# Seven staged weight slices, a third engine for a normalization, split first loads, an early Exp, and a new written order

## The chip, the cores and the metric

The kernel runs on one core of a Trainium2 chip. The core has five engines that run side by side, each through its own list of instructions in order: TensorE (PE in the rows; PEld is its loading of weights), VectorE (DVE), ScalarE (ACT), GpSimd (POOL) and SyncE (SP), which here does nothing but issue DMAs. They meet at semaphores. The metric is the time of one execution on the device in microseconds (us), the median of several runs.

## The reference, cut to what matters

```python
# q, k, v: (4 batches, 12 heads, 448 rows, 64), float32
scores = q @ k.T / 8, causal mask, softmax       # per batch and head
x = attn @ v, heads put side by side             # (4, 448, 768)
mixed = real(fft(fft(x, axis=1), axis=2))
u = x + mixed
un = (u - mean(u)) / sqrt(var(u) + 1e-6)         # per row of 768
out = u + maximum(un @ w_ch1, 0) @ w_ch2         # w_ch1: 768 x 3072, w_ch2: 3072 x 768
```

The weights arrive as 64-bit floats; each pair of 32-bit words is made into one float32 on the chip.

## The kernel before

The program is a list of some 4,300 units: a matmul group, a copy, a DMA issue and so on. The functions of `tile_kernel` add the units; each names what it reads and writes. Two tables written out by hand then fix everything: `RUN` is the order in which the units are issued, and `BY` gives each unit's engine (P, V, S, G, D for PE, DVE, ACT, POOL and a DMA on SP's queue). `BANK` and `BUF` give the PSUM bank or buffer of each new tile. So each engine's list is its part of `RUN`, and each waits only where a unit needs what another engine has not finished.

The work falls in three stages that overlap:

- **Attention and DFT** (to about 260 us). `attend` takes one pair of heads at a time, 24 pairs: load `raw` (q and k) and `v`; scale q to `qs`; masks and scores into PSUM (PE, lines 581 and 588); row minima `mn` (DVE, 600); exponentials `p` with their sums (ACT, 608); reciprocals `ri` (DVE, 616 and 620); normalizing `p` (638, 640, 642 on ACT, DVE or POOL); four groups of transposes (PE, 654), each copied to `pa`; then the product with v (PE, 664), copied to `xt`. After six pairs a batch is whole: `fold` makes sums and differences `f` of `xt` (DVE, POOL), and `dft` multiplies them by tables (PE, 722 and 739), adds `xt` transposed (PE, 765), which gives `u` (DVE, 775). `un`, the normalized `u`, is made at line 801 from the row's mean and from a factor that POOL works out in two small operations (791 and 792), transposed (811) and written to DRAM.
- **First layer** (F1, 1,512 matmuls at line 1014, to about 547 us). Strassen's scheme: seven products of half-size blocks. `weights` turns raw 64-bit weights into float32 `w32` (ACT 833, 837, 850; DVE 856, 860); `split` makes a high and a low part of each block (copies at 487 and 489, differences at 876), `combine` the sums of blocks (882). Three matmuls (high-high, high-low, low-high) stand for one. Results go to DRAM.
- **Second layer** (F2, 1,764 matmuls at line 1184, to the end). Twelve slices of w_ch2 pass in the same way. Those listed in `EARLY` are split during F1 already and kept in DRAM (`w2`, stores at 1144); F2 only fetches them. The others are made during F2. DVE adds each product to `acc` or `ue` (1200).

At the start eleven dummy matmuls (`warm`, line 502) run while the first data come in. `W_FROM = 10` lets the first weight load start once the v of pair 10 has been loaded.

## Time and profile before

| | us |
|---|---|
| median of 3 runs (lowest to highest) | 862.75 (862.38 to 864.58) |
| the profiled execution, its own time | 862.93 |
| its span, first to last instruction | 861.2 |
| PE busy in the span | 846.0 |
| DVE, ACT, POOL busy | 726.9, 542.9, 452.9 |

Between the span and the execution's own time lie 1.7 us. PE is busy 98% of the span. Matmuls are pipelined and their ends are modelled, so a busy PE may still lose a little between matmuls; the number of matmuls in equal windows tells of that. [...]

### The profile page before, as it was taken

The page shows a single profiled execution, that of the slowest core. Times are in us where ns is not written, and L with a number is a line of the kernel's source. Part 1 is how long each engine was busy: PE and PEld are TensorE (multiplying, and loading weights), DVE is VectorE, ACT ScalarE, POOL GpSimd, SP SyncE. Part 2 cuts the span into 40 slices and gives each one's busy share as a digit, 9 for nine tenths or more (in the row PEclk, how much of TensorE's full clock was granted, in tenths as well). Part 3 has the DMA queues.
Part 4 walks back from the last instruction along what each step waited for, and adds up shares of the span by engine and source line. Part 5 has one row for each costly group of instructions (what it writes and reads, how often), then busy time and mean ns, then how long its engine had stood idle before and what let it go on. Part 6 is the DMA issues. An engine that isn't in the chain of part 4 may idle for free. (4 is left out here: it accounts for less than half of the span.)

```text
span 861.2 us, 15758 instructions
## 1 busy us (share of the span) xinstructions
PE 846.0 (98%) x5407; PEld 754.7 (88%) x5407; DVE 726.9 (84%) x1335; ACT 542.9 (63%) x1120; POOL 452.9 (53%) x466
## 2 busy tenths in 40 slices
PE   8999999999999999999999999999999999999998
PEld 4677677686788899899999988999999999999998
DVE  5889999888999996898877659899799999987653
ACT  5888999979788977787777456584443421332220
POOL 1654756668270234345453342446646666797675
PEclk9999999999999999999999999999999999999999
DMA  6535847656596687888778668574474385447332
GB/s 225 171 118 180 299 135 214 210 171 182 168 294 215 210 276 264 259 274 282 261 247 275 223 205 280 186 245 140 137 228 131 119 275 157 129 122 236 115 133 91
DMA packets 121359, 174.02 MB, mean 202 GB/s; under 512 B 21696, under 2 KB 98240, under 8 KB 121280
## 3 DMA queue, kind: packets, MB, share of 16 engines
q1 hardware_dynamic: 121280, 173.03, 62.3%
q8 instruction: 42, 0.69, 0.3%
q14 instruction: 37, 0.30, 0.1%
HBM read 112.83 MB, written 60.16 MB: 201 GB/s over the span
## 5 line engine op out<-in xcount | busy, mean ns | idle before, releaser
L1184 PE MATMUL psum<-wa,w 128*128 128x384 f32 x1050 | 208.6, 336 | 0.5 <-DVE acc L1200 0.3
L1184 PEld LDWEIGHTS psum<-wa,w 128*128 128x128 f32 x1050 | 184.0, 188 | 1.7 <-issue 0.6
L1184 PE MATMUL psum<-wb,w 128*128 128x384 f32 x714 | 149.6, 336 | 0.0
L1184 PEld LDWEIGHTS psum<-wb,w 128*128 128x128 f32 x714 | 125.9, 188 | 0.2 <-DVE ue L1200 0.2
L1014 PE MATMUL psum<-0t,w 128*128 128x448 f32 x432 | 107.9, 366 | 2.1 <-DVE c L489 0.8
L1014 PE MATMUL psum<-1t,w 128*128 128x448 f32 x432 | 102.4, 363 | 0.9 <-ACT c L487 0.5
L850 ACT ACTIVATE w<-w 128x768 int8<-128x768 f32 x48 | 94.4, 1967 | 0.5
L876 POOL TENSOR_TENSOR w<-ws,w 128x384 fp32r<-128x384 f32 x57 | 64.5, 1139 | 53.4 <-DVE w L489 24.2
L608 ACT ACTIVATE p<-psum,mn 128x256 f32<-128x256 f32 (+3 forms) x168 | 83.2, 510 | 10.4 <-DVE mn L600 10.0
L1014 PEld LDWEIGHTS psum<-0t,w 128*128 128x128 f32 x432 | 79.9, 188 | 10.9 <-ACT c L487 3.3
L1014 PEld LDWEIGHTS psum<-1t,w 128*128 128x128 f32 x432 | 80.4, 187 | 8.2 <-ACT c L487 1.3
L487 ACT CAST w<-us 128x384 fp32r<-128x384 f32 x65 | 32.5, 516 | 77.5 <-PE psum L1184 49.0
L1200 DVE TENSOR_TENSOR acc<-psum,acc 128x384 f32<-128x384 f32 x96 | 51.1, 550 | 26.1 <-PE psum L1184 25.2
L487 ACT CAST w<-ws 128x384 fp32r<-128x384 f32 x81 | 39.9, 515 | 52.1 <-DVE ws L882 22.2
L876 POOL TENSOR_TENSOR w<-us,w 128x384 fp32r<-128x384 f32 x45 | 52.5, 1174 | 36.3 <-ACT w L487 22.4
L600 DVE TENSOR_REDUCE mn<-psum 128x1 f32<-128x448 f32 (+3 forms) x96 | 62.0, 665 | 10.6 <-PE psum L588 8.1
L588 PE MATMUL psum<-raw,qs 64*128 64x384 f32 (+3 forms) x336 | 66.5, 430 | 0.1
L642 POOL TENSOR_TENSOR p<-p,ri 128x128 f32<-128x128 f32 (+3 forms) x61 | 37.5, 635 | 39.7 <-DVE ri L620 35.2
L1040 DVE TENSOR_TENSOR c<-psum,c 128x448 f32<-128x448 f32 x69 | 42.7, 620 | 15.8 <-PE psum L1014 8.9
L1014 PE MATMUL psum<-ue,w 128*128 128x448 f32 x216 | 54.1, 365 | 0.0
L654 PEld LDWEIGHTS psum<-cst,p 128*128 128x128 f32 x384 | 42.6, 141 | 12.6 <-issue 3.8
L860 DVE SCALAR_TENSOR_TENSOR w<-w,w 128x768 uint32<-128x768 uint32 x48 | 49.6, 1033 | 4.5 <-ACT w L850 3.9
(195 smaller groups left out, 1844.7 us busy)
## 6 DMA issues: line engine op xcount, KB each, us to landing
w<-in_w_dram SPq DMA_DIRECT2D x48, 768.0 KB, 4.9
h<-c SPq DMA_DIRECT2D x93, 224.0 KB, 2.9
w<-us SPq DMA_DIRECT2D x84, 192.0 KB, 2.7
raw<-in_qk_dram SPq DMA_DIRECT2D x23, 480.0 KB, 4.4
c<-h SPq DMA_DIRECT2D x56, 192.0 KB, 2.9
us<-h SPq DMA_DIRECT2D x56, 192.0 KB, 3.4
wa<-w SPq DMA_DIRECT2D x23, 384.0 KB, 5.1
wb<-w SPq DMA_DIRECT2D x19, 384.0 KB, 4.9
```

What stands on the lines that cost most here:

```text
L487: nc.scalar.copy(out=out, in_=in_)
L588: nc.tensor.matmul(out=T[ps][:, at[r]:at[r] + n], lhsT=T[qs][s, q0:q0 + 128], rhs=T[raw][s, QW:QW + n], start=False, stop=y == len(rows) - ...
L600: nc.vector.tensor_reduce(out=z, in_=x, axis=AX, op=ALU.min)
L608: nc.scalar.activation(out=T[pb][:, PO[rr]:PO[rr] + n], in_=T[ps][:, c0:c0 + n], func=ACTF.Exp, scale=-1.0, bias=T[mn][:, rr:rr + 1], accu ...
L654: nc.tensor.transpose(T[ps][:, 128 * k:128 * k + 128], T[pb][:, e:e + 128], T["cst", 0][:, 0:128])
L850: nc.scalar.activation(out=T[w].bitcast(I8)[:, :, 3], in_=T[w][:, :, 1].bitcast(F32), func=ACTF.Prelu, scale=SIGN_SCALE, alpha=SIGN_ALPHA)
L860: nc.vector.scalar_tensor_tensor(out=T[w32], in0=T[w32], scalar=3, in1=T[w][:, :, int(join)], op0=ALU.logical_shift_left, op1=ALU.bitwise_or)
L876: (nc.gpsimd if eng == "G" else nc.vector).tensor_tensor(out=lo(), in0=src(), in1=hi(), op=ALU.subtract)
L1014: nc.tensor.matmul(out=T[ps][:, 0:S], lhsT=w[:, a, t], rhs=T[us[t]][:, b], start=first and k == 0, stop=last and k == 8, skip_group_check= ...
L1040: nc.vector.tensor_tensor(out=T[z], in0=T[ps][:, 0:S], in1=T[z], op=ALU.add)
L1184: nc.tensor.matmul(out=T[ps][:, 0:384], lhsT=T[hb][:, a, y], rhs=T[z][:, b], start=first and y + v == 0, stop=last and y == n - 1 and v == ...
L1200: nc.vector.tensor_tensor(out=x, in0=T[ps][:, 0:384], in1=x, op=ALU.add)
```

## The change

- `EARLY` has a seventh slice, 5, in F1: it is split there, stored in 14 DMAs and fetched in seven during F2. It had been made in F2.
- `un` may be made on ACT, as one Identity with a scale and a bias per row. In the new `BY` 10 of the 16 are: two of batch 0, one of batch 1, three of batch 2, all four of batch 3. For it POOL works out two more numbers per row, for all 16: four small operations in place of two.
- The first pair's q and k come in four pieces and its q is scaled in two; the constants come, and are cast, in two pieces.
- An Exp of one number per partition stands first on ACT. Nothing uses its result.
- `W_FROM` is 0: the first weight load may start after the first v.
- `RUN`, `BY`, `BANK` and `BUF` are new throughout. PE does the same 1,005 units. Counted in the tables, DVE has 1,311 units (1,335 before), ACT 949 (951), POOL 474 (445), and SP 612 DMAs (588).

```diff
@@ constants of the plan
-ALONE, WIN, REST, EARLY, JOIN = 3, 3, (0,) * 7, (0, 3, 6, 8, 9, 11), ()
+ALONE, WIN, REST, EARLY, JOIN = 3, 3, (0,) * 7, (0, 3, 5, 6, 8, 9, 11), ()
-C_FROM, W_FROM, N_WARM = 0, 10, 11
+C_FROM, W_FROM, N_WARM = 0, 0, 11
@@ RUN (BY, BANK and BUF alike)
-    0, 6, 2, 5, 43, 89, 1, 7, 126, 8, 3, 9, 16, 10, 13, 20, 45, 14, 17, 11, 46, 172, 44, 12, 15, 91, 49, 18, 21, 19,
+    0, 4, 2, 6, 9, 8, 7, 10, 1, 11, 49, 95, 133, 96, 12, 5, 3, 13, 15, 14, 22, 19, 16, 26, 18, 21, 51, 132, 23, 50,
...
@@ consts
-        def f():
-            nc.sync.dma_start(out=T["cst", 0], in_=cc)
-        add("D", dma(128 * 4 * CW), -2498.5, f, wr=[("cst", 0)], phase="A")
-
-        def f(eng):
-            copy(eng, T["bfc", 0], T["cst", 0])
-        add(("S", "V", "G"), (acts(CW), dve(CW, 1.92), gps(CW)), -1898, f, rd=[("cst", 0)], wr=[("bfc", 0)], phase="A")
+        for key, c0, c1, p in (("b", 128, CW, -2498.5), ("a", 0, 128, -2300)):
+            def f(c0=c0, c1=c1):
+                nc.sync.dma_start(out=T["cst", 0][:, c0:c1], in_=cc[:, c0:c1])
+            add("D", dma(512 * (c1 - c0)), p, f, wr=[("cst", 0, key)], phase="A")
+
+            def f(eng, c0=c0, c1=c1):
+                copy(eng, T["bfc", 0][:, c0:c1], T["cst", 0][:, c0:c1])
+            n = c1 - c0
+            add(("S", "V", "G"), (acts(n), dve(n, 1.92), gps(n)), p + 600, f, rd=[("cst", 0, key)], wr=[("bfc", 0, key)], phase="A")
-        add("G", 80, 1000, f, wr=[("eps", 0)], phase="A")
+            nc.gpsimd.memset(T["eps", 0][:, 2:3], -1.0)
+        add("G", 80, -2600, f, wr=[("eps", 0)], phase="A")
+
+        def f():
+            nc.scalar.activation(out=T["eps", 0][:, 3:4], in_=T["eps", 0][:, 0:1], func=ACTF.Exp)
+        add("S", 1500, -2599, f, rd=[("eps", 0)], wr=[("eps", 0, "e")], phase="A")
@@ attend, loading and scaling
-            load(QW, QW + S, [(*raw, "k")], base - 2500)
-            load(0, QW, [(*raw, "q")], base - 2499)
+            load(QW, QW + 256, [(*raw, "k")], base - 2500)
+            load(0, 256, [(*raw, "q")], base - 2499)
+            load(256, QW, [(*raw, "q1")], base - 2498)
+            load(QW + 256, QW + S, [(*raw, "k1")], base - 2497)
-            load(0, QW + S, [(*raw, "q"), (*raw, "k")], base - 2500)
+            load(0, QW + S, [(*raw, z) for z in ("q", "k", "q1", "k1")], base - 2500)
-        def f(eng):
-            if eng == "S":
-                nc.scalar.mul(T[qs], T[raw][:, 0:QW], -0.125)
-            else:
-                (nc.gpsimd if eng == "G" else nc.vector).tensor_scalar(
-                    out=T[qs], in0=T[raw][:, 0:QW], scalar1=-0.125, scalar2=None, op0=ALU.mult)
-        add(("S", "V", "G"), (acts(QW), dve(QW, 1.92), gps(QW) + 216), sp, f, rd=[(*raw, "q")], wr=[qs], phase="A")
+        for k, (c0, c1) in enumerate(((0, 256), (256, QW)) if i == 0 else ((0, QW),)):
+            def f(eng, c0=c0, c1=c1):
+                x, z = T[raw][:, c0:c1], T[qs][:, c0:c1]
+                if eng == "S":
+                    nc.scalar.mul(z, x, -0.125)
+                else:
+                    (nc.gpsimd if eng == "G" else nc.vector).tensor_scalar(out=z, in0=x, scalar1=-0.125, scalar2=None, op0=ALU.mult)
+            n = c1 - c0
+            add(("S", "V", "G"), (acts(n), dve(n, 1.92), gps(n) + 216), sp + k, f, rd=[(*raw, "q1" if k else "q"), *([] if i == 0 else [(*raw, "q1")])],
+                wr=[(*qs, k)], phase="A")
@@ dft, normalization
-                    nc.gpsimd.tensor_tensor(out=T[st6][0:w, 14:15], in0=T[st6][0:w, 13:14], in1=T["eps", 0][0:w, 0:1], op=ALU.add)
-                    nc.gpsimd.tensor_tensor(out=T[st6][0:w, 14:15], in0=T[st6][0:w, 14:15], in1=T["eps", 0][0:w, 1:2], op=ALU.pow)
-                add("G", 785, pr[0], f, rd=[mv, ("eps", 0)], wr=[rs], phase="Q")
+                    r = T[st6][0:w, 14:15]
+                    nc.gpsimd.tensor_tensor(out=r, in0=T[st6][0:w, 13:14], in1=T["eps", 0][0:w, 0:1], op=ALU.add)
+                    nc.gpsimd.tensor_tensor(out=r, in0=r, in1=T["eps", 0][0:w, 1:2], op=ALU.pow)
+                    nc.gpsimd.tensor_tensor(out=T[st6][0:w, 15:16], in0=T[st6][0:w, 12:13], in1=r, op=ALU.mult)
+                    nc.gpsimd.tensor_tensor(out=T[st6][0:w, 15:16], in0=T[st6][0:w, 15:16], in1=T["eps", 0][0:w, 2:3], op=ALU.mult)
+                add("G", 1300, pr[0], f, rd=[mv, ("eps", 0)], wr=[rs], phase="Q")
+                    if eng == "S":
+                        nc.scalar.activation(
+                            out=T[un][0:w], in_=T[u][0:w], func=ACTF.Identity, scale=T[st6][0:w, 14:15], bias=T[st6][0:w, 15:16])
+                        return
-                add(("V", "G"), (590, 3150), pr[0], f, rd=[*ua, mv, rs], wr=[un], phase="Q")
+                add(("V", "G", "S"), (590, 3150, acts(768) + 93), pr[0], f, rd=[*ua, mv, rs], wr=[un], phase="Q")
```

Where the order moves things, three places. The first is the start of ACT's list: up to the first pair's exponentials (`p`, from scores in `psum` and minima `mn`).

Before:

```order
L608 ACT_TABLE_LOAD
L608 ACTIVATE p,sum<-psum,mn 128x256
L608 ACTIVATE p,sum<-psum,mn 128x128 x2
L608 ACTIVATE p,sum<-psum,mn 128x256
L608 ACTIVATE p,sum<-psum,mn 128x384 x2
L608 ACTIVATE p,sum<-psum,mn 128x448 x2
L638 ACTIVATE p<-p,ri 128x256
```

With the change:

```order
L524 ACT_TABLE_LOAD
L524 ACTIVATE eps<-eps 128x1
L567 ACTIVATE qs<-raw 128x256 x2
L622 ACTIVATE p,sum<-psum,mn 128x128
L622 ACTIVATE p,sum<-psum,mn 128x256 x2
L622 ACTIVATE p,sum<-psum,mn 128x128
L622 ACTIVATE p,sum<-psum,mn 128x384
L622 ACTIVATE p,sum<-psum,mn 128x448
```

The table load stood in front of the first exponential, behind the minima that this one waits for; now it stands in front of the Exp on `eps`, which waits for a POOL memset alone, and two scalings of q follow it.

The second place is on PE, around the product with v of pair 8 (`pa,v`), behind the last transposes of that pair (`cst,p`); the L581 rows of the masks that stand between are left out.

Before:

```order
L588 MATMUL psum<-raw,qs 128x128 x2
L588 MATMUL psum<-raw,qs 128x256 x2
L654 MATMUL psum<-cst,p 128x128 x12
...
L588 MATMUL psum<-raw,qs 128x448
L654 MATMUL psum<-cst,p 128x128 x4
L664 MATMUL psum<-pa,v 64x384 x2
L664 MATMUL psum<-pa,v 64x64 x2
```

With the change:

```order
L668 MATMUL psum<-cst,p 128x128 x12
L832 MATMUL psum<-cst,un 128x112 x3
...
L601 MATMUL psum<-raw,qs 128x128 x2
L601 MATMUL psum<-raw,qs 128x256 x2
L678 MATMUL psum<-pa,v 64x384 x2
L678 MATMUL psum<-pa,v 64x64 x2
```

One group of four transposes stood just ahead of the product with v. Now transposes of `un` and a whole unit of scores (`raw,qs`, with its masks) stand between.

The third is on PE too, from behind the last product with v (pair 23; with the change, from behind a first group of `un` transposes too) to the first DFT matmul of batch 3 (`cd,f`), which needs that product's copies `xt` and their sums `f`; `ue,w` and `0t,w` are F1 matmuls.

Before:

```order
L1014 MATMUL psum<-ue_2425,w_1026 128x448 x3
L765 MATMUL psum<-cst,xt_2372 112x128 x3
L1014 MATMUL psum<-0t_3022,w_2942 128x448 x3
L1014 MATMUL psum<-ue_2612,w_1026 128x448 x3
L1014 MATMUL psum<-0t_3027,w_2942 128x448 x3
L765 MATMUL psum<-cst,xt_2372 113x128 x3
L811 MATMUL psum<-cst,un 128x112 x3
L1014 MATMUL psum<-0t_3035,w_2942 128x448 x3
L722 MATMUL psum<-cd,f_2729 113x194
```

With the change:

```order
L1035 MATMUL psum<-ue_1697,w_916 128x448 x3
L1035 MATMUL psum<-ue_2582,w_906 128x448 x3
L832 MATMUL psum<-cst,un 128x112 x3
L1035 MATMUL psum<-ue_2466,w_916 128x448 x3
L1035 MATMUL psum<-ue_2588,w_916 128x448 x3
L1035 MATMUL psum<-0t_3033,w_2985 128x448 x3
L779 MATMUL psum<-cst,xt_2434 112x128 x6
L779 MATMUL psum<-cst,xt_2434 113x128 x3
L1035 MATMUL psum<-0t_3043,w_2985 128x448 x3
L1035 MATMUL psum<-0t_3054,w_2985 128x448 x3
L1035 MATMUL psum<-0t_3068,w_2936 128x448 x3
L736 MATMUL psum<-cd,f_2774 113x194
```

Ahead of the first transposes of `xt` (`cst,xt`) stood one group of three F1 matmuls; now five such groups and two of `un` transposes stand there, and up to the first `cd,f` there are eight groups of three F1 matmuls where there were five.

## Rows read from the trace of the kernel before

**Rows 1.** Page, part 1: engine, busy us (share of the span), instructions.

```profile
PE 846.0 (98%) x5407; PEld 754.7 (88%) x5407; DVE 726.9 (84%) x1335; ACT 542.9 (63%) x1120; POOL 452.9 (53%) x466
```

**Rows 2.** Windows: us, then busy PE, PEld, DVE, ACT, POOL, clock, DMA share, GB/s.

```profile
0.00:16.00 16.00, 13.23 (x77) 6.20 (x78) 7.89 (x20) 7.29 (x24) 0.59 (x5) 1.00 0.81 274
16.00:45.00 29.00, 28.16 (x307) 19.77 (x307) 25.28 (x51) 25.39 (x88) 16.59 (x24) 1.00 0.47 149
...
80.00:124.00 44.00, 42.00 (x439) 29.23 (x438) 42.51 (x97) 41.78 (x118) 27.75 (x39) 1.00 0.67 224
...
214.00:262.00 48.00, 45.85 (x292) 38.33 (x291) 46.14 (x93) 40.25 (x80) 22.18 (x25) 1.00 0.77 236
262.00:300.00 38.00, 37.21 (x179) 32.61 (x178) 37.00 (x69) 34.36 (x61) 6.36 (x5) 1.00 0.62 202
300.00:500.00 200.00, 199.05 (x991) 184.61 (x990) 158.96 (x271) 141.26 (x190) 80.86 (x73) 1.00 0.78 260
500.00:560.00 60.00, 58.39 (x294) 53.60 (x294) 48.84 (x90) 37.33 (x60) 22.55 (x21) 1.00 0.74 230
560.00:850.00 290.00, 289.50 (x1666) 288.07 (x1665) 245.36 (x414) 106.71 (x203) 195.56 (x167) 1.00 0.52 162
850.00:861.20 11.20, 7.56 (x44) 7.24 (x42) 3.61 (x7) 0.00 (x0) 1.04 (x2) 0.94 0.39 140
```

**Rows 3.** Timeline, first 16 us: start, us, engine, line, operation, count, idle before.

```profile
1.18 4.87 PE L502 MATMUL psum<-xt 128*128 128x512 bf16 x11 [1.18 <-DVE xt L496]
...
6.59 0.52 PEld L588 LDWEIGHTS psum<-raw,qs 64*128 64x128 f32 x8 [0.32 <-DMA raw<-in_qk_dram]
...
8.70 1.28 ACT L608 ACT_TABLE_LOAD   x1 [8.70 <-DVE mn L600]
...
10.96 0.30 PE L581 MATMUL psum<-bfc 64*128 64x128 bf16 x6 [0.64 <-ACT p L608]
...
13.50 0.19 PE L581 MATMUL psum<-bfc 128*128 128x64 bf16 x1 [0.67 <-ACT p L608]
```

**Rows 4.** Waits of PE, 80 to 125 us: total, times, longest.

```profile
PE psum L664 <- ACT pa L487: 0.5, 1, 0.5
...
PE psum L664 <- DVE pa L489: 0.4, 1, 0.4
```

**Rows 5.** Timeline of PE, 218 to 262 us.

```profile
220.18 1.98 PE L664 MATMUL psum<-pa,v 128*64 128x384 f32 x28
...
224.05 0.59 PE L765 MATMUL psum<-cst,xt 128*112 128x128 f32 x3 [1.08 <-ACT xt L487]
...
228.76 2.54 PE L722 MATMUL psum<-cd,f 128*113 128x194 f32 x14 [0.40 <-DVE f L701]
```

**Rows 6.** Windows of 20 us, two of them.

```profile
260.00:280.00 20.00, 19.39 (x95) 17.15 (x94) 19.67 (x39) 17.26 (x30) 1.47 (x1) 1.00 0.63 203
360.00:380.00 20.00, 20.00 (x102) 18.58 (x101) 16.97 (x28) 16.79 (x24) 7.66 (x7) 1.00 0.83 267
```

**Rows 7.** Tile un: count, ns min/median/max, first and last start.

```profile
L801 DVE TENSOR_SCALAR un<-u,st x16: 642/673/1370, 73.0 to 254.8; 112x768 f32<-112x768 f32 x12, 113x768 f32<-113x768 f32 x4
```

**Rows 8.** Line 791, the same columns.

```profile
L791 POOL TENSOR_TENSOR st<-st,eps x16: 191/192/845, 70.8 to 253.8; 112x1 f32<-112x1 f32 x12, 113x1 f32<-113x1 f32 x4
```

**Rows 9.** Lines by form, ACT and DVE: count, busy us, mean ns, idle before.

```profile
L833 ACT ACTIVATE w<-w 128x768 f32<-128x768 f32 x48 | 44.1, 919 | 12.2 <-POOL ws L882 3.3 <-DVE ws L882 3.2 <-POOL w L876 2.1
...
L860 DVE SCALAR_TENSOR_TENSOR w<-w,w 128x768 uint32<-128x768 uint32 x48 | 49.6, 1033 | 4.5 <-ACT w L850 3.9
```

**Rows 10.** Line 876: count, ns min/median/max.

```profile
L876 DVE TENSOR_TENSOR w<-ws,w x59: 543/552/1385, 218.4 to 824.2; 128x384 fp32r<-128x384 f32 x59
```

**Rows 11.** Line 1200, the same columns.

```profile
L1200 DVE TENSOR_TENSOR acc<-psum,acc x96: 541/548/559, 592.6 to 857.6; 128x384 f32<-128x384 f32 x96
```

**Rows 12.** Waits of the DMA queue: total, times, longest.

```profile
SPq L1144 <- POOL w L876: 75.7, 24, 7.7
```

More of the change, by code (lines that the diff above doesn't have):

```diff
@@ new lines @@
+BUF = (
+    "13000200021121213000011011101221020120112012121002103100120212110020110000102211222113021100301000210201110121"
+    "12220001113100020113012120320101211011100023102210010200013211121011110120001311103200101111232302220132011221"
+    "03100110100120112110121003010201121200001311021020030231013213201004010223124501230123012301213020202671321001"
+    "13012301230121100460104275320111403062124073120121102202012010312003120312321403050126104311201112100410302132"
+    "01002231103752121267500210012120010313202130130111043021142276200112201203501231052611042301032032102311201201"
+    "01203400147210311000323413210230120221100212035220160507110413213030123023021120001120023014126721301130321223"
+    "101230201200001400032154063521201212240220712203205402611720012003a46511301872e92fd1304gc0b6319123410761015012"
+    "13021101224103762120013512407640102232005217123113015012720034310052165c8bgae10044d370f287cb0ga410213510720140"
+    "23065106732520133020621721023451004372101104620513064122074105210102032461257302e256f9d0312131196354db80ce3011"
+    "0212054760021233512234134021072026504200223511037104310107620524371021361106043232120710101545af7g2ab12007044c"
+    "8g9e162f5d3101373212617311002620156140221123720156433200221100727620035121405201202730236410021337216574310022"
+    "502601040110061253167")
@@ L590, in f @@
                             start=False, stop=y == len(rows) - 1, skip_group_check=True)
-            add("PE", SC_COST[0 if tail else len(rows)], p0, f, rd=[qs, (*raw, "k"), ("bfc", 0)], wr=banks, phase="A", mode="F" if tail else "H")
+            add("PE", SC_COST[0 if tail else len(rows)], p0, f, rd=[*([(*qs, 0), (*raw, "k")] if i or k == 0 else [(*qs, 0), (*qs, 1), (*raw, "k"), (*raw, "k1")]), *([(*raw, "k1")] if i else []),
+                ("bfc", 0, "b"), *([("bfc", 0, "a")] if tail else [])], wr=banks, phase="A", mode="F" if tail else "H")
             for y, r in enumerate(rows):
@@ L654, in f @@
                     nc.tensor.transpose(T[ps][:, 128 * k:128 * k + 128], T[pb][:, e:e + 128], T["cst", 0][:, 0:128])
-            add("PE", TR_COST, p0, f, rd=[*[(*pb, r, "n") for r in {r for r, _ in blocks}], ("cst", 0)], wr=[ps], phase="A")
+            add("PE", TR_COST, p0, f, rd=[*[(*pb, r, "n") for r in {r for r, _ in blocks}], ("cst", 0, "a")], wr=[ps], phase="A")
             def f(eng, ps=ps, g=g):
```

102 lines of the change are left out of this document (45 added, 57 removed), and 457 rows, old and new, of the table RUN.

## Prediction

> **What bounds the kernel now.** I read the page's part 1 first: PE is busy 846.0 of the span's 861.2 us, so all that a new order can win back is PE's idle time, 15.2 us, and what PE loses between matmuls while it counts as busy [rows 1]. The arithmetic on PE is unchanged, 1,005 units.
>
> Windows by stage say where the idle time lies (stretch less PE busy): 2.8 us in the first 16, 0.8 from 16 to 45, 2.0 from 80 to 124, 2.2 from 214 to 262, 0.8 from 262 to 300, 0.95 from 300 to 500, 1.6 from 500 to 560, 0.5 from 560 to 850, and 3.6 at the end [rows 2]. The reader is to see two things. The stretches that lose most are those where another engine is full: ACT 41.78 and DVE 42.51 of 44 from 80 to 124, DVE 46.14 of 48 and 37.00 of 38 from 214 to 300. And F2 is nearly free of loss, though DVE is busy there for 245.36 of 290.
>
> Busy hides more. A window of 20 us in mid F1 holds 102 matmuls, 0.196 us each; the one from 260 to 280 holds 95, so it loses 7 x 0.196 = 1.4 us, where its idle time is 0.61 [rows 6]. The 179 matmuls from 262 to 300 fill 35.1 of 38 us: 2.9 lost, 0.8 of it as idle [rows 2].
>
> The end of 3.6 us (last product, last sum, last store) is written as before, and the wait of 1.18 ahead of the dummies too [rows 3].
>
> **The change, part by part.**
>
> *The early Exp.* ACT's first work was the table load, 1.28 us from 8.70 on, behind the first minima, with the exponentials behind it [rows 3]. From 8.70 to 16 ACT is busy 7.29 of 7.30 us, so what it starts late it ends late. PE waits for those exponentials twice, 0.64 and 0.67 [rows 3]. Now the load waits for a memset only and lies under the dummies, which hold PE until 6.05. Worth 1.28 at most by this way; the normalization of the first pair also passes DVE, whose new order puts one more minimum ahead of it, so I take 1.2, with bounds 0.5 and 1.6 (1.6 is all of PE's idle in these 16 us but the first 1.18). [...]
>
> *First loads in pieces.* PE waited for raw until 6.59, just behind the dummies' end [rows 3]. Of the bytes ahead of the first scores, 720 KB of q, constants and k become 490 KB. The dummies hide all of it: 0, up to 0.1 won. If the second pieces land no sooner than k did, their scaling on ACT ends about when the second unit of scores wants it; without that cover it costs under 0.5, which the bound of 0.5 above takes in.
>
> *First weight load moved ahead.* Two loads of 768 KB now stand on SP's queue behind the raw tiles of the first pairs, and land from 16 to 45 us, where the DMA engines are busy 0.47 [rows 2]. Hidden: 0. If not, a raw tile of pair 5 or 9 is late, each 480 KB behind 1.5 MB.
>
> *Normalization on ACT.* Ten instructions of 0.673 leave DVE [rows 7]: 6.7 us, of which seven, 4.7, in batches 2 and 3, the last of them at 254.8. On ACT the nearest row is another 768-wide operation, 0.919 [rows 9]; ten cost 9.2. From 214 to 262, where at least four of them fall, ACT is idle 7.75 us. POOL's two more products cost 2 x 0.19 per row block [rows 8], 6.1 us in all, and make each `un` some 0.4 us later; the transposes of `un` are far enough behind for that.
>
> *The order.* Around the product of pair 8, PE waited 0.5 for `pa` on ACT, and for pair 10 0.4 for `pa` on DVE [rows 4]. The new order puts un transposes and a unit of scores between for pair 8, and three units of scores for pair 10 where one and a group of transposes stood: over a microsecond more PE work in each place. I take 0.9; bounds 0 and 2.0, all idle time of that stretch.
>
> Behind the last product with v, which begins at 220.18, PE waits 1.08 for `xt` and 0.40 for `f` [rows 5]. The new order has nine more F1 matmuls of 0.196 there, 1.8 us, besides 15 transposes for nine: more than 1.48. Both waits go: 1.5. From 262 to 300 DVE is the limit, and 4.7 us of its work have gone just before. It can't return more than the 2.9 lost; between 0 and 2.9 I take the middle, 1.4.
>
> *The seventh slice.* Upper bound of its DVE work: four operations of 1.033 [rows 9] and 18 of 0.552 [rows 10], 14 us. It leaves F2, where PE idles 0.5 in all [rows 2]: I take 0.2, bounds 0 and 0.5. It goes to the stretch from 300 to 500, where DVE has 41 us free and ACT 59: 0. Its 14 stores and 7 fetches of 192 and 384 KB are hidden where no PE wait is for a DMA.
>
> *500 to 560.* All is rewritten there and DVE has less to do; 0.3 of the 1.6, bounds -1 and 1.6. *New waits.* An order that is new throughout makes its own: 0.5 lost, bounds 0 and 3.
>
> Sum: 1.2 + 0.9 + 1.5 + 1.4 + 0.2 + 0.3 - 0.5 = 5.0. The profiled execution took 862.93, the median is 862.75; from the median, **857.8 us**.
>
> **The rivals.**
>
> *Given back on DVE.* POOL gets 29 more units of about 0.97 (452.9 by 466 [rows 1]) and 32 small ones. DVE's differences of two SBUF tiles take 0.543 to 1.385 [rows 10], those with one input in PSUM 0.541 to 0.559 [rows 11]: something lengthens the first kind alone. [...] If each of the 29 lengthens one DVE instruction by 0.83, that is 24 us of DVE, some 3.6 of it in the 130 us where DVE or ACT is full: the 1.4 go, and most of the 0.9 and 0.3 with them: 862.75 - 1.2 - 1.5 + 0.5 = 860.5, within 860.2 and 863.5.
>
> *ACT becomes the bound (slower).* ACT had 2.2 us free from 80 to 124, and two normalizations more in the stretch before and in it. If the four of batch 3 and three of batch 2 lie on the way of PE with their whole 0.92, PE loses 6.4 and wins 2.1 at the start and around pair 8: 867. It decides once ACT's free 7.75 us from 214 to 262 are used up, which takes another 4 us of moved work beside the four. ACT's units, 949 where there were 951, speak against it.
>
> *SP's queue (slower or the same).* SP waits in order: 75.7 us in 24 waits for POOL's low parts ahead of the stores at 1144, 3.2 each [rows 12]. Fourteen more, all behind one another near 300 us, hold back the loads behind them by up to 44 us in sum; a weight late by 3 us would make 861, by 10 868. Against it: PE waits for no DMA behind 6.59 today.
>
> *Won throughout.* If every bound falls well: 1.6 + 2.0 + 2.2 + 2.9 + 1.6 + 0.5 = 10.8, 852.
>
> **How the numbers follow.** Forecast (855 to 860.1) 0.48; won throughout (850 to 855) 0.18; given back (860.2 to 863.5) 0.20; ACT or SP slower 0.14, of which a little ends within 0.3%. About 0.3%, 2.6 us, is what a measurement of this kernel can tell from no change, so faster is below 860.2 and slower above 865.3: 0.66, 0.22, 0.12. The range 851 to 863.5 leaves out a part of "won throughout" and all that is slower; the likeliest case's own range is 855 to 860.1.
>
> **What would show it.** Right: a table load before 3 us and the first exponential near 8.7; no wait for L608 on PE before 12 us; no waits of 1.08 and 0.40 near 220; DVE below 0.95 from 214 to 300 with some 184 or more matmuls in 262 to 300. Wrong: PE waits for `un` or for ACT's copies from 190 to 260; DVE busy as before in spite of ten operations less, with two-input differences longer than 0.65 on average; PE waiting for a weight or `h` near 300 to 340; new idle time of several us in F1.

## The result and the profile after

| | before | with the change |
|---|---|---|
| median, runs of both side by side (us) | 862.71 (862.38 to 864.58, 4 runs) | 851.54 (851.52 to 852.41, 4 runs) |
| profiled execution, its span | 862.93, 861.2 | 852.41, 850.6 |

The ratio is 0.9869, with a 95% interval of 0.9852 to 0.9886: 11.2 us faster, where 5.0 were forecast. The time lies just inside the range, and nearest to the rival that everything is won. The profiled execution of the changed kernel is the longest of its four; the other three took 851.5.

The page's part 1 of the changed kernel answers to [rows 1]:

```profile
PE 840.7 (99%) x5407; PEld 755.7 (89%) x5407; DVE 730.8 (86%) x1311; ACT 544.3 (64%) x1118; POOL 495.7 (58%) x528
```

PE's idle time went from 15.2 to 9.9 us, and its busy time from 846.0 to 840.7 for the same 5,407 matmuls. So half of the 10.6 us of span, 5.3, came out of time that counts as busy. DVE has 24 instructions fewer and is busy 3.9 us longer.

Windows over the stretches of [rows 2], with the same columns:

```profile
0.00:16.00 16.00, 13.91 (x100) 7.46 (x102) 9.49 (x22) 10.24 (x35) 3.33 (x9) 1.00 0.71 234
...
80.00:124.00 44.00, 43.72 (x450) 31.44 (x450) 41.42 (x89) 43.37 (x124) 34.17 (x47) 1.00 0.67 209
...
214.00:262.00 48.00, 46.97 (x273) 40.98 (x268) 45.54 (x87) 44.18 (x77) 25.27 (x33) 1.00 0.83 251
262.00:300.00 38.00, 37.67 (x184) 33.98 (x185) 37.34 (x65) 33.31 (x60) 12.65 (x11) 1.00 0.66 225
300.00:500.00 200.00, 198.49 (x989) 184.76 (x988) 167.29 (x275) 145.60 (x193) 97.39 (x86) 1.00 0.82 274
500.00:560.00 60.00, 60.00 (x317) 57.08 (x316) 56.64 (x98) 40.72 (x71) 27.14 (x24) 1.00 0.82 261
```

PE idles 0.3 from 80 to 124 (2.0 before) and nothing from 500 to 560 (1.6). The engines that feed PE are not emptier for it: from 80 to 124 ACT is fuller by 1.6 (43.37 of 44) and DVE emptier by 1.1, and from 500 to 560 DVE is fuller by 7.8 (56.64 of 60).

The timeline of the first 12 us, beside [rows 3]:

```profile
0.72 1.28 ACT L524 ACT_TABLE_LOAD   x1 [0.72 <-PEq L1374]
...
1.17 4.42 PE L503 MATMUL psum<-xt 128*128 128x512 bf16 x11 [1.17 <-DVE xt L497]
...
5.71 0.90 PE L601 MATMUL psum<-raw,qs 64*128 64x128 f32 x8
...
7.78 0.37 ACT L622 ACTIVATE p<-psum,mn 128x128 f32<-128x128 f32 x1 [1.80 <-DVE mn L614]
...
11.85 0.64 PE L601 MATMUL psum<-raw,qs 128*128 128x448 f32 x1 [0.63 <-POOL qs L569]
```

The table load lies under the dummies, the first exponential comes at 7.78 (9.98 before, where the load ended), and PE's two waits for exponentials are gone. A wait of 0.63 for a scaling on POOL is new in this profile.

Of PE's waits from 80 to 125 us there is one row, beside [rows 4]:

```profile
PE psum L668 <- ACT p L622: 0.3, 1, 0.3
```

The waits from 214 to 262 us, beside [rows 5], have one row too:

```profile
PE psum L753 <- ACT bs L488: 0.3, 1, 0.3
```

All four waits of the old rows are gone. The tile `un`, beside [rows 7] (count, ns min/median/max, first and last start), is now made on two engines:

```profile
L819 ACT ACTIVATE un<-u,st x10: 975/1030/1068, 71.4 to 248.5; 112x768 f32<-112x768 f32 x7, 113x768 f32<-113x768 f32 x3
L822 DVE TENSOR_SCALAR un<-u,st x6: 627/672/1284, 81.3 to 202.9; 112x768 f32<-112x768 f32 x5, 113x768 f32<-113x768 f32 x1
```

DVE's differences of two SBUF tiles, beside [rows 10], before and with the change (count, busy us, mean ns, idle before):

```profile
L876 DVE TENSOR_TENSOR w<-ws,w 128x384 fp32r<-128x384 f32 x59 | 37.7, 646 | 2.7 <-ACT w L487 2.5
L897 DVE TENSOR_TENSOR w<-ws,w 128x384 fp32r<-128x384 f32 x58 | 45.1, 782 | 6.1 <-ACT w L488 5.7
```

**Where the time came from.** Each group of matmuls is given its shortest usual duration (three of F1 0.60, a product with v 1.88, and so on), and these are summed in PE's order: the work done, 825.5 us in all. What PE's clock shows beyond it is what PE has lost so far. The table is worked out from all matmuls of each trace; in the kernel before, 40, 100, 200, 220, 300, 480, 520 and 720 us of work are done at 47, 113, 217, 241, 325, 508, 550 and 751 us.

```
us lost when so much work is done
work   before   e1    e5    e11   e13  | changed  e15   e4    e9    e14
  40     6.9    6.1   7.7   7.4   6.9  |   3.5    3.3   3.9   4.6   4.1
 100    12.5   11.8  15.1  15.9  12.5  |   6.9    6.8   7.6   8.6  11.3
 200    17.4   16.6  22.5  20.4  17.4  |  12.2   12.1  15.5  14.8  16.7
 220    21.2   20.4  26.3  24.2  20.9  |  13.6   13.5  17.2  16.5  18.1
 300    25.3   24.4  33.5  28.8  25.4  |  17.8   17.8  22.2  21.5  22.3
 480    28.1   28.0  36.3  31.5  28.5  |  19.7   18.9  23.2  22.7  23.3
 520    30.3   30.2  38.5  33.7  30.8  |  20.0   19.1  23.4  22.9  23.6
 720    31.3   31.6  39.9  35.1  32.2  |  20.1   19.3  23.5  23.0  23.7
 end    35.7   35.3  43.6  38.8  35.9  |  25.1   23.3  27.6  27.2  28.5
```

By the change PE wins 3.4 over the first 40 us of work, 2.2 up to 100, 2.4 from 200 to 220 and 1.9 from 480 to 520; all else together gives 0.7. From 220 to 300 it wins nothing: the old kernel loses 4.1 there and the changed one 4.2.

How far executions differ can be read from the table too. The changed kernel, e15, e4, e9 and e14 do the same work up to 40 us, and have lost 3.3 to 4.6 there; and from 300 to 480 the first profile of the changed kernel loses 1.9, the other four 1.0 to 1.2.

### The profile page after: what moved, and what is told of

It is laid out like the page before. It is cut to its first block, busy times and chain, and to the rows that moved or that the text cites. A ratio compares the mean times of both kernels' runs of the same rounds, so it can differ in the third digit from the quotient of the medians.

```text
span 850.6 us, 15801 instructions
## 1 busy us (share of the span) xinstructions
PE 840.7 (99%) x5407; PEld 755.7 (89%) x5407; DVE 730.8 (86%) x1311; ACT 544.3 (64%) x1118; POOL 495.7 (58%) x528
## 4 chain that ended last, share of the span: by engine, by line
PE 52%; DVE 1%; DMA 1%; ACT 0%; issue 0%; DVEq 0%
PE psum L1205 35%; PE psum L1035 17%; DMA w<-in_w_dram 1%; DVE ue L1221 0%; DVE us L490 0%; DVE c L1061 0%; ACT w L871 0%; DVE ws L903 0%; DVE w L897 0%; ACT w L854 0%; ACT w L858 0%; DVE w L881 0%; DVE acc L1221 0%; DVE us L897 0%; DVE w L490 0%
## 5 line engine op out<-in xcount | busy, mean ns | idle before, releaser
L1035 PE MATMUL psum<-0t,w 128*128 128x448 f32 x432 | 105.7, 364 | 0.8 <-ACT c L488 0.8
L897 POOL TENSOR_TENSOR w<-ws,w 128x384 fp32r<-128x384 f32 x58 | 68.5, 1186 | 58.0 <-DVE w L490 29.7
L622 ACT ACTIVATE p<-psum,mn 128x128 f32<-128x128 f32 (+3 forms) x168 | 82.9, 512 | 11.7 <-DVE mn L614 10.7
L488 ACT CAST w<-ws 128x384 fp32r<-128x384 f32 x88 | 44.6, 516 | 60.7 <-PE psum L1205 22.5
L601 PE MATMUL psum<-raw,qs 64*128 64x128 f32 (+3 forms) x336 | 66.0, 430 | 0.6 <-POOL qs L569 0.6
L488 ACT CAST w<-c 128x384 fp32r<-128x384 f32 x44 | 22.3, 515 | 63.5 <-PE psum L1205 44.8
L881 DVE SCALAR_TENSOR_TENSOR w<-w,w 128x768 uint32<-128x768 uint32 x48 | 55.8, 1163 | 2.6 <-ACT w L871 2.0
L897 POOL TENSOR_TENSOR w<-us,w 128x384 fp32r<-128x384 f32 x39 | 43.7, 1124 | 23.4 <-ACT w L488 17.8
L897 POOL TENSOR_TENSOR w<-c,w 128x384 fp32r<-128x384 f32 x40 | 47.2, 1186 | 15.3 <-ACT w L488 11.2
L656 POOL TENSOR_TENSOR p<-p,ri 128x256 f32<-128x256 f32 (+3 forms) x61 | 41.2, 695 | 22.6 <-DVE ri L634 16.7
```

What stands on the lines that cost most here:

```text
L488: nc.scalar.copy(out=out, in_=in_)
L601: nc.tensor.matmul(out=T[ps][:, at[r]:at[r] + n], lhsT=T[qs][s, q0:q0 + 128], rhs=T[raw][s, QW:QW + n], start=False, stop=y == len(rows) - ...
L622: nc.scalar.activation(out=T[pb][:, PO[rr]:PO[rr] + n], in_=T[ps][:, c0:c0 + n], func=ACTF.Exp, scale=-1.0, bias=T[mn][:, rr:rr + 1], accu ...
L656: nc.gpsimd.tensor_tensor(out=x, in0=x, in1=z.to_broadcast([128, KE[r]]), op=ALU.mult)
L881: nc.vector.scalar_tensor_tensor(out=T[w32], in0=T[w32], scalar=3, in1=T[w][:, :, int(join)], op0=ALU.logical_shift_left, op1=ALU.bitwise_or)
L897: (nc.gpsimd if eng == "G" else nc.vector).tensor_tensor(out=lo(), in0=src(), in1=hi(), op=ALU.subtract)
```

## The experiments

**e1: the early Exp alone, in the kernel before.**

```diff
+        def f():
+            nc.scalar.activation(out=T["eps", 0][:, 3:4], in_=T["eps", 0][:, 0:1], func=ACTF.Exp)
+        add("S", 1500, -2599, f, rd=[("eps", 0)], wr=[("eps", 0, "e")], phase="A")
```

> The kernel before, with the Exp of one number put first on ACT and its memset first on POOL, and nothing else changed. Theory A (the single edits carry the gain, each at its own place): the table load of 1.28 leaves the chain at 8.70, the first exponential starts at 8.7 in place of 9.99, and the kernel ends 1.2 us earlier, 861.5 (bounds 860.9 to 862.2). Theory B (the new order carries the gain, and the old order's later waits take back what the start wins): the first exponential is as early, but the time is within 0.4 of 862.7.

Measured 861.38 (859.72 to 862.9), ratio 0.9982 (0.9973 to 0.9991), against 863.05 beside it. In the profile 0.8 is ahead from 40 us of work on, and all but 0.1 is lost again between 360 and 380. That execution took 862.65, the second longest of the eleven, so the profile doesn't show what the median won.

**e2: the changed kernel without the Exp**, the first pair's two scalings on DVE.

```diff
-            nc.scalar.activation(out=T["eps", 0][:, 3:4], in_=T["eps", 0][:, 0:1], func=ACTF.Exp)
```

> The changed kernel without the early Exp, and with the two scalings of the first q on DVE, so that ACT's first instruction is again the first exponential with the table load in front of it. Theory A: 1.2 to 1.3 us slower than 851.5, 852.8. Theory B: the start is late by 1.3 us but the order takes half or more of it back behind, 851.5 to 852.1.

Measured 851.99 (851.63 to 852.37), ratio 0.9872 (0.9859 to 0.9886): 0.45 above the changed kernel, inside the error. Compared matmul by matmul (both run the same ones in the same order), its profile is 1.3 later than that of the changed kernel at 47 us, though its dummies end 0.14 earlier; 0.75 of it is a wait of PE for `p` on ACT at 13.77, which the changed kernel has not. So the Exp wins about a microsecond at the start. ACT's timeline has the table load back in front of the exponentials:

```profile
7.63 1.28 ACT L608 ACT_TABLE_LOAD   x1 [7.63 <-DVE mn L600]
8.92 0.37 ACT L608 ACTIVATE p<-psum,mn 128x128 f32<-128x128 f32 x1
```

**e3: the changed kernel with whole first loads.**

```diff
-            load(QW, QW + 256, [(*raw, "k")], base - 2500)
-            load(0, 256, [(*raw, "q")], base - 2499)
-            load(256, QW, [(*raw, "q1")], base - 2498)
-            load(QW + 256, QW + S, [(*raw, "k1")], base - 2497)
+            load(QW, QW + S, [(*raw, "k"), (*raw, "k1")], base - 2500)
+            load(0, QW, [(*raw, "q"), (*raw, "q1")], base - 2499)
```

> The changed kernel with the first q, the first k and the constants loaded whole again (constants, q, k in that order); casts and scalings still in two. The trace after shows the first scores 0.9 us earlier than before (5.71 against 6.59), where the prediction gave the pieces nothing. Theory A: the first scores are back near 6.5 and the kernel takes 0.9 more, 852.4. Theory B: the dummies hide it as predicted, or the order behind takes it back: within 0.2 of 851.5.

Measured 851.82 (851.5 to 852.13), ratio 0.987 (0.9857 to 0.9884). In the profile it is 1.0 later at 40 us of work and 0.2 at 480. But its dummies ended at 6.05, as in the kernel before, and in the changed kernel's profile at 5.59, which no edit made. In e4, which has the pieces and dummies to 6.01, the first scores begin at 6.12 and take 0.90; here they begin at 6.29 and take 1.30, why is not shown. So where the dummies run that long the pieces bring the scores forward by 0.2, and no run shows that they win more, at the start or at the end.

**e4: the ten normalizations back on DVE, in the new order.**

```diff
@@ BY, ten entries of un
-S S S S S S S S S S
+V V V V V V V V V V
```

> The changed kernel with the ten normalizations back on DVE, all else and the order as it is. Theory A: DVE, which is 95 to 98% busy from 214 to 300, gets 4.7 us back there and 2.0 ahead of it; PE loses 1.4 to 3 us between 60 and 300, 853 to 854.5. Theory B: the gain of those stretches is due to the order; within 0.5 of 851.5.

Measured 856.49 (854.48 to 857.45), ratio 0.9919 (0.9904 to 0.9933): 4.95 lost. The profiled execution took 854.85, the second shortest of the five, and shows 2.4 beside the first profile of the changed kernel, 4.2 beside that of e15. Compared matmul by matmul, 2.5 of it are lost between 200 and 214 us and 1.1 more by 300. The first loss lies at one place, which the timeline of e4 shows:

```profile
203.63 1.39 POOL L656 TENSOR_TENSOR p<-p,ri 128x256 f32<-128x256 f32 x2
...
204.01 3.62 DVE L822 TENSOR_SCALAR un<-u,st 112x768 f32<-112x768 f32 x1
...
204.98 2.23 POOL L698 TENSOR_TENSOR d<-xt 128x448 f32<-128x448 f32 x2
...
207.88 0.54 DVE L789 TENSOR_TENSOR u<-psum,ad 112x384 f32<-112x384 f32 x1
...
208.47 0.26 PE L594 MATMUL psum<-bfc 64*128 64x128 bf16 x4 [2.03 <-DVE u L789]
```

A normalization of 0.67 takes 3.62 while four POOL operations on two inputs run, one behind the other, until 207.2. DVE's `u` is late by that, and PE waits 2.03. This normalization is one of the six that stay on DVE in the changed kernel too; there it starts at 202.86, in the second half of POOL's first pair, and takes 1.28.

**e5: the ten normalizations on ACT, in the old order.**

```diff
@@ BY of the kernel before, ten entries of un; POOL's two more operations on all 16 go with it
-V V V V V V V V V V
+S S S S S S S S S S
```

> The kernel before, with the same ten normalizations on ACT as the changed kernel has, and POOL's four small operations for the factor; the written order is the old one. Theory A (the relief of DVE is worth its time by itself): DVE loses 6.7 us of work, ACT takes 9.2, and the stretch from 262 to 300 wins 1.4 to 2.9 and the one from 80 to 124 up to 1: the time is 858.8 to 861.2. Theory B (the relief is worth something only in an order written for it; in the changed kernel, taking it back cost 4.9 us of the median because that order counts on it): within 1 us of 862.7, or slower where ACT's copies wait behind a normalization.

Measured 870.53 (869.8 to 870.92), ratio 1.0088 (1.0074 to 1.0102): 7.7 slower. PE's waits from 60 to 265 us, the longest:

```profile
PE psum L819 <- ACT un L806: 1.8, 4, 0.7
PE psum L819 <- ACT c L1056: 1.4, 1, 1.4
PE psum L766 <- ACT ub L487: 1.1, 1, 1.1
```

In the old order `un` stands in ACT's list where it suited DVE: it takes 1.03 there and has copies of F1 and of `ub` in front of and behind it, on which PE waits.

**e6 and e7: slice 5 without its preparation**, from F2 of the kernel before and from F1 of the changed one.

```diff
@@ e6; in e7 the preparation returns at once where k is 5
+        if k == 5:
+            at(t - W2_LEAD, fetch, k, F0 + t - FETCH_LEAD)
@@ both
-                nc.sync.dma_start(out=T[z].bitcast(F32), in_=dr["w2"][k, W2B.index(name)])
+                nc.sync.dma_start(out=T[z].bitcast(F32), in_=dr["w2"][6 if k == 5 else k, W2B.index(name)])
```

> The kernel before, with the preparation of slice 5 left out of F2: its seven blocks are fetched from the place of slice 6, so that part of the output is computed from the wrong slice. Prediction on record: F2 wins 0.2 (0 to 0.5) by it, so the time is 862.2 to 862.7. Rival: DVE's work in F2 delays PE by more than the idle time of PE shows, and the time falls by 1 us or more, below 861.7.

> The changed kernel, with the preparation of slice 5 in F1 and its 14 stores left out: F2 fetches the blocks of slice 6 in their place, so that part of the output is computed from the wrong slice. Prediction on record: the slice costs F1 nothing (DVE has 41 us free from 300 to 500, ACT 59), so the time stays at 851.5 within 0.5. Rival: it costs F1 by way of the DMA queue or of DVE, the idle times of PE near 318, 392 and 486 us (0.46, 0.50, 0.56) go with it, and the time falls to about 850.

e6 measured 868.97 (867.98 to 869.79), ratio 1.0069 (1.0057 to 1.0082), and tells nothing of F2: PE waits once, 5.13 at 640.36. The profile names no releaser. Likely it is a block: from 600 to 645 us the queue of fetches had waited 6.0 us in all for PE to free their buffers, and those issued behind 628 landed 6.3 to 8.0 us later. The wait costs more than itself: in the 5 us behind it the granted clock reads 0.51 and PE does 15 matmuls, in the next 5 it reads 1.00 and PE does 31 (windows as in [rows 2]):

```profile
635.00:640.00 5.00, 0.22 (x2) 0.00 (x0) 1.24 (x3) 0.43 (x1) 0.60 (x1) 0.81 1.13 333
640.00:645.00 5.00, 4.64 (x15) 4.68 (x16) 4.79 (x10) 1.86 (x3) 1.35 (x2) 0.51 0.47 160
645.00:650.00 5.00, 5.00 (x31) 5.00 (x30) 4.14 (x7) 2.17 (x5) 2.75 (x4) 1.00 0.58 175
```

e7 measured 852.58 (852.19 to 852.94), ratio 0.9881 (0.9867 to 0.9894). Without the slice F1 is not faster, so no cost in F1 is seen, as predicted. The time is 1.0 above the changed kernel's, though, where within 0.5 was expected; compared matmul by matmul, its profile is 0.9 behind by 300 us, ahead of nearly all the slice's work, and 1.0 at 500. Why is not shown.

e6 shows something else. In the kernel before, PE waits 0.47 at 533.67 for a difference on DVE, and in e6 it doesn't, though slice 5 has no work near. The timelines of the kernel before have there, POOL, DVE and then PE:

```profile
532.18 1.02 POOL L876 TENSOR_TENSOR w<-w,w 128x384 fp32r<-128x384 f32 x1 [10.12 <-ACT w L487]
532.19 1.43 DVE L876 TENSOR_TENSOR w<-w,w 128x384 fp32r<-128x384 f32 x1
...
533.67 0.47 PE L1014 MATMUL psum<-1110_3495,w 128*128 128x448 f32 x1 [0.47 <-DVE w L876]
```

The same two operations in the timeline of e6:

```profile
531.84 0.56 DVE L865 TENSOR_TENSOR w<-w,w 128x384 fp32r<-128x384 f32 x1
531.84 1.44 POOL L865 TENSOR_TENSOR w<-w,w 128x384 fp32r<-128x384 f32 x1 [10.12 <-ACT w L476]
```

Both start within 0.01 us, and one is lengthened: once DVE by 0.88 (1.43 for 0.55), once POOL by 0.42 (1.44 for 1.02).

**e8 and e11: products moved in the old order.** Both move the products with v of pairs 8 and 10 behind other work; e8 also moves a unit of scores of pair 13 ahead.

```diff
@@ RUN of the kernel before, PE's units
-(x, 8) (at, (0,1,0)) (pt, (9,1)) (at, (0,1,1))
+(at, (0,1,0)) (pt, (9,1)) (at, (0,1,1)) (x, 8)
-(x, 10) (sc, (13,2)) (pt, (11,3))
+(sc, (13,2)) (pt, (11,3)) (x, 10)
@@ e8 only
-(pt, (10,2)) (pt, (10,1)) (pt, (10,3)) (sc, (13,0))
+(sc, (13,0)) (pt, (10,2)) (pt, (10,1)) (pt, (10,3))
```

> The kernel before with three moves in PE's order alone: the product with v of pair 8 goes behind two groups of transposes of un and one of p, that of pair 10 behind a unit of scores and one group of transposes of p, and a unit of scores of pair 13 goes ahead of the transposes of pair 10. Theory A (the waits of 0.51, 0.42 and 0.42 are local, and work between ends them): 1.2 to 1.4 us won by 110 us and kept, the time 861.3 to 861.8. Theory B (DVE and ACT, full from 80 to 124, set the pace, and the waits come back some us later): no gain kept behind 124 us, the time 862.4 to 863.

> The kernel before with two moves of e8 alone: the product with v of pair 8 behind two groups of transposes of un and one of p, that of pair 10 behind a unit of scores and one group of transposes of p. The unit of scores of pair 13, which went into a PSUM bank whose scores were still to be read, stays where it was. Theory A (the loss of e8 came from that unit): 0.5 to 0.9 won, 861.8 to 862.3. Theory B (a product moved later holds back DVE's and ACT's work that hangs on it, and PE then waits for un, as it did in e8 for 1.80 at 88.3): 1 to 5 us lost, 863.7 to 868.

e8 measured 869.26 (868.23 to 869.72), ratio 1.0072 (1.0058 to 1.0085); its extra unit overwrites scores of pair 12 that were still to be read. PE idles there for 2.2 of the 10 us from 80 on and for 1.8 of those from 110 on, and the granted clock reads 0.85 from 90 to 100 us and 0.83 from 110 to 120, so part of its loss may be the clock's. In e11 it reads 1.00 from 60 to 130. e11 measured 866.51 (865.11 to 868.91), ratio 1.0048 (1.0037 to 1.006): 3.9 slower. PE's waits from 60 to 125 us in e11:

```profile
PE psum L801 <- DVE un L791: 1.8, 1, 1.8
PE psum L571 <- ACT p L598: 1.8, 1, 1.8
PE psum L644 <- DVE p L630: 0.4, 1, 0.4
```

The 0.51 and 0.42 for `pa` are gone. In their place PE stands 1.8 in front of transposes whose `un` is not ready, now that they come earlier, and 1.8 for exponentials behind the later product.

**e9: e4, with the one held-up normalization on ACT.**

```diff
@@ BY, the entry of un of batch 2, second in its pair
-V
+S
```

> The changed kernel with the ten normalizations back on DVE, as in e4 (856.5 us), but the one of batch 2 that took 3.62 us there, from 204.01 on, while four operations of POOL on two inputs ran, goes to ACT (in the changed kernel it is on DVE and takes 1.28). Theory A (a single instruction of DVE held up by POOL made most of the loss, PE's wait of 2.03 us at 208.47): that wait goes and the time falls to 853.5 to 854.5. Theory B (the sum of DVE's work makes it, ten times 0.67): one in ten moved brings 0.5, the time is 855.7 to 856.5.

Measured 854.07 (853.14 to 854.48), ratio 0.9897 (0.9882 to 0.9911): 2.4 of the 4.95 come back by this one instruction. PE has no wait like that of 2.03 there, and compared matmul by matmul the profile loses 0.9 between 200 and 214 us, where e4 loses 2.5. The time is that of theory A. No run moved POOL's operations: that they lengthened the instruction rests on the overlap in e4.

**e10 and e12: the scaling behind the new wait of 0.63 moved to DVE**, and then two dummies fewer.

```diff
@@ BY, the scaling of the third pair's q
-G
+V
@@ e12 only
-C_FROM, W_FROM, N_WARM = 0, 0, 11
+C_FROM, W_FROM, N_WARM = 0, 0, 9
```

> The changed kernel with the scaling of the third pair's q on DVE (0.42) in place of POOL (1.50). PE waits 0.63 for it at 11.85. Theory A (PE sets the pace behind the front): the wait goes and 0.3 to 0.6 stay to the end, 850.9 to 851.3. Theory B (time won at the front is given back near 390 us, as between e2, e3 and the changed kernel): the time stays at 851.5 within 0.3.

> As e10, with nine dummy matmuls in place of eleven. Each of the first nine takes 0.43, and from about 5 us on a dummy takes 0.22. Theory A (PE begins its scores as soon as the dummies end and the first pieces have landed, near 5.1): the first scores begin 0.3 to 0.4 earlier, at full rate, and the time is 0 to 0.4 below e10. Theory B (without the last dummies PE is still at the slower rate, or waits for the pieces): the scores take longer, and the time is the same as e10 or up to 0.5 above.

Measured 851.64 (850.65 to 852.1) and 851.71 (851.18 to 852.24), ratios 0.9871 (0.9858 to 0.9883) and 0.9873 (0.986 to 0.9886): no gain. In both profiles PE instead waits 1.3 and 1.4 for the second pair's scaling, near 9.5. e14 has the same wait, 1.29 at 9.31, without this edit, so the edit is not its cause. That scaling itself waits for its data, in e10:

```profile
8.91 0.43 DVE L569 TENSOR_SCALAR qs<-raw 128x512 f32<-128x512 f32 x1 [1.54 <-DMA raw<-in_qk_dram]
```

So where PE stands in the first 12 us differs with the landing of the first loads, and e10 and e12 could not test the wait of 0.63.

**e13: the two waits behind the last product with v, filled in the old order.**

```diff
@@ RUN of the kernel before, PE's units
-(an, (3,0,0)) (h0, (0,a),2,0) (h0, (0,d),1,2)
+(h0, (0,d),1,2) (an, (3,0,0)) (h0, (0,a),2,0)
-(ay, (3,0,a,1),0) (ay, (3,0,b,1),0) (ay, (3,0,b,1),1) (an, (3,0,1))
+(an, (3,0,1)) (ay, (3,0,a,1),0) (ay, (3,0,b,1),0) (ay, (3,0,b,1),1)
```

> The kernel before with two moves in PE's order behind the last product with v: three F1 matmuls, 0.60, go ahead of the first product that waits 1.08 for xt at 224.05, and one product with xt, 0.33, ahead of the one that waits 0.40 for f at 228.76. Theory A (these waits end by their own clock, so that work put into them is won): PE's waits there fall to 0.5 and 0.1, and 0.9 are kept to the end: 861.8. Theory B (what hangs on the moved work is held back in turn, or DVE, full from 214 to 300, sets the pace): not more than 0.3 is kept by 300 us, 862.4 to 863.

Measured 862.86 (862.12 to 863.21), ratio 0.9999 (0.999 to 1.0008): nothing. Its window beside [rows 2]:

```profile
214.00:262.00 48.00, 46.41 (x292) 38.03 (x291) 46.15 (x93) 40.05 (x80) 22.13 (x25) 1.00 0.78 237
```

The two waits fell to 0.47 and 0.12, and PE's idle time in the stretch by 0.56 us. But PE finished the same 292 matmuls in it as before, and DVE's 46.15 is the same too. The time went from idle to busy and nowhere else.

**e14: the fillers of the new order taken out**, ahead of the product of pair 8 and, in part, of pair 10.

```diff
@@ RUN of the changed kernel, PE's units
-(at, (0,1,0)) (sc, (10,0)) (x, 8)
+(x, 8) (at, (0,1,0)) (sc, (10,0))
-(sc, (13,2)) (x, 10)
+(x, 10) (sc, (13,2))
```

> The changed kernel, with a group of transposes of un and a unit of scores put behind the product with v of pair 8 instead of ahead of it, and one unit of scores behind that of pair 10. Theory A (the fillers end the waits that stood there before, 0.51 and 0.42): PE waits about 0.5 for pa ahead of pair 8's product again, up to 0.4 ahead of pair 10's, and 0.5 to 0.9 are lost to the end: 852.0 to 852.4. Theory B (the copies of pa are early enough by the order as a whole): no wait over 0.2 there, 851.5 within 0.3.

Measured 855.64 (854.24 to 856.19), ratio 0.9914 (0.9901 to 0.9928): 4.1 lost, where 0.5 to 0.9 were expected. PE's waits from 60 to 125 us, of which the changed kernel has only the last:

```profile
PE psum L658 <- DVE p L644: 0.7, 1, 0.7
PE psum L584 <- ACT p L612: 0.5, 1, 0.5
PE psum L668 <- ACT pa L478: 0.5, 1, 0.5
PE psum L658 <- ACT p L612: 0.3, 1, 0.3
```

The wait for `pa` is back, as theory A has it. But the scores that were put off also make their exponentials, and so the `p` of later transposes, late, and these cost more than the wait itself.

**e15: the changed kernel once more.** There is no edit.

> The changed kernel unchanged, for a second profile. Theory A (the wait of 0.50 at 392.09 for a copy of DVE, behind a weight that landed 6.9 us after its issue, belongs to this order): it is there again, and the longest landing of a weight between 300 and 400 us is again 6 to 7 us. Theory B (the landing differs from one execution to the next): it is gone or lies elsewhere. The dummies' end, 5.53 in the first profile, lies between 4.9 and 6.0 by either. Time 851.5 within 0.4.

Measured 851.42 (850.61 to 852.25), ratio 0.9868 (0.9854 to 0.9881); the profiled span is 848.8. PE's timeline begins:

```profile
1.17 3.85 PE L503 MATMUL psum<-xt 128*128 128x512 bf16 x11 [1.17 <-DVE xt L497]
4.96 0.34 PE L594 MATMUL psum<-bfc 64*128 64x128 bf16 x8
...
7.10 0.92 PE L601 MATMUL psum<-raw,qs 64*128 64x384 f32 x4 [0.98 <-DMA raw<-in_qk_dram]
```

The dummies end earlier than in the first profile, and PE waits 0.98 for the first pair's raw data instead; the wait of 0.63 for POOL is not there. The wait of 0.50 at 392.09 of the first profile is not there either, though the longest landing of a weight is again 6.8. Theory B: such a loss differs from one execution to the next.

Compared matmul by matmul, e15 runs level with the first profile, within 0.2, from 12 to 380 us, and is 0.8 ahead from 400 on and 1.8 at 840. e2 and e3 are 0.9 and 1.1 behind the first profile at 380 us, and 0.1 and 0.2 at 400. So what looks like time given back near 390 is time that the first profile itself lost there. Beside e15 they stay behind, with spans of 849.8 and 850.3 against 848.8.

## Why the prediction was wrong

The sign was right, and most of what was to show it came; the size was off by more than a factor of two. What failed is the sum itself: it took PE's waits in the old order as separate holes, each worth what it shows, and each edit as worth the same in any order. The term that failed most is the 1.4 from 262 to 300, for the normalizations that leave DVE. That the time ends beside "won throughout" is chance: its largest bound, 2.9, gave nothing, and the first 40 us, pair 8, the last product and 500 to 560 each gave more than their bounds.

- *The order around pairs 8 and 10: 0.9, bounds 0 and 2.0, "all idle time of that stretch".* The change won 2.2 between 40 and 100 us of work (47 to 113 us in the kernel before), above the upper bound. That bound was idle time alone, of which 1.7 went from 80 to 124; PE also loses in time that counts as busy. It is no local gain: moving the products alone lost 3.9 (e11), and moving three fillers back in the new order lost 4.1 (e14). The waits in both runs fit one reading: each unit on PE starts a chain over DVE and ACT, and its place sets when all of that chain is ready.
- *Behind the last product with v: 1.5, "both waits go".* They went, and 2.4 came from that stretch. But filling 0.9 of them in the old order won nothing (e13), so the 1.5 was not the price of those waits. That DVE sets the pace there, busy for 46 of 48 us in [rows 2] as in e13, fits the equal matmul counts, but was not tried by itself.
- *From 262 to 300: 1.4, for the normalizations on ACT.* By the table nothing was won from 220 to 300 us of work, 241 to 325 in the kernel before. The 184 matmuls in the window came, but the changed kernel is some 7.5 us ahead by then and does other work in it. What the normalizations are worth lies elsewhere, and the price was wrong. It rests on "ten instructions of 0.673 leave DVE", a median. The row of [rows 7] also shows 1370 as the longest, and e4 has one of 3616. Undone in the new order, the move costs 4.95, of which 2.4 hang on one DVE instruction, near 204 us, that takes 3.62 beside four POOL operations (e4, e9). Made in the old order, it loses 7.7 (e5). The 0.919 that stood for an `un` on ACT was 1.03.
- *DVE beside POOL* was thought of for differences of two SBUF tiles alone, and as a reason against the change. That each of POOL's 29 more units lengthens one of them by 0.83 was the author's estimate, from the longest and the median of [rows 10]. No run shows it: of these differences on DVE 51 take over 0.7 us in the kernel before (line 876) and 59 in the changed one (line 897). `un` on DVE has one SBUF input and takes 3.62 for 0.67 beside POOL in e4, which speaks for taking it off DVE. The rival "given back on DVE" did happen in its first half: DVE's differences `w<-ws` took 0.782 on average, where they took 0.646, and DVE is busier with fewer instructions. The second half did not: PE's idle time fell all the same from 80 to 124, 214 to 300 and 500 to 560 us.
- *Early Exp and front: 1.2; pieces: 0.* By 40 us of work 3.4 were won, where the bound was 1.6. The Exp was priced well: about 1 at the start (e2), and 1.7 at the end in the old order (e1, interval 0.8 to 2.3). The pieces show 0.2 (e3), and their 0.3 in the median is less than the runs can tell. But "the dummies, which hold PE until 6.05" were taken as fixed: by the same rows they end at 5.59 in the changed kernel's profile and at 5.02 in e15, which is no work of the change and 0.5 of the 3.4. The rest of it no run explains.
- *The seventh slice: 0.2 and nothing in F1.* e7 shows no cost in F1; for F2 no run tells.
- *500 to 560: 0.3 of 1.6.* Between 480 and 520 us of work 1.9 were won. One of the waits there, 0.47, stood behind a DVE difference of 1.43 that began 0.01 us after one on POOL; in e6 that difference takes 0.56, and the wait is gone. For the rest no experiment stands, and its cause is argued only: a new order, DVE busier than before, and no wait.
- *New waits: −0.5.* The new order has some, 0.77 at 262, 0.46 at 318 and 0.56 at 486 us, in e15 as well; that of 0.63 at 11.85 us is not in e15. They lie within the balance above.
- *ACT becomes the bound* is what e5 shows, at 870.5: a rival of the old order, not of the new one. *SP's queue* left no wait of PE for a DMA behind the first pairs; the 0.50 at 392 in the first profile stands behind a weight that landed 6.9 us after its issue. That rival also read a wrong row, and the section on the kernel before names the wrong line: 1144 is not where the blocks are stored but where F2 loads `h`; the stores, at 1100, waited 5.8 us for POOL in the kernel before and 12.1 in the changed one.

Of the signs named ahead, the table load, PE's waits for exponentials, both waits near 220 and the 184 matmuls came as said; the first exponential came at 7.78, 0.9 before the time named. DVE below 0.95 from 214 to 300 did not come: 45.54 and 37.34 of 86 us are 0.96. And one sign of being wrong came: DVE is busy as before, with two-input differences of 0.782 on average, above 0.65.

What stays open: how much of the 11.2 belongs to which part cannot be added up, since parts such as the normalizations are worth something else beside the others. The removals from the changed kernel (0.45, 0.3, 4.95 and 4.1 in e2, e3, e4 and e14) are no shares of it.

## What to carry to other kernels

Where every engine's list is written by hand and two helpers are full, a wait need not be a hole to be filled: price a new order by all that it makes early or late, PE's slow busy time included, and set a wide upper bound. An edit that moves work to another engine has to be judged with the order it comes in, since the same ten moves lost 7.7 in one order and were worth 5 in the other. Before a median stands for an operation on DVE, look at its longest one (3.62 for a median of 0.67 in e4), and at what POOL does then. And before two profiles are compared, see where each stands among the times of its kernel: here one kernel's two profiles differ by 1.8 us.
